# Attention and a low-rank mixer on one core: scores three key blocks at a time, with a PSUM bank pair taken from other uses

## The chip, the core and the metric

The kernel runs on one core of a Trainium2 chip. A core has TensorE (PE in the profile; its weight loads are shown apart as PEld), VectorE (DVE), ScalarE (ACT), GpSimd (POOL) and SyncE (SP, which here only issues transfers). TensorE writes its results to PSUM, and VectorE or ScalarE must read them out of there; this reading out is called an eviction below. The metric is the time of one execution on the device, in microseconds (us). Before the change it is 588.72 us, the median of three runs (587.74 to 589.25).

## What is computed

Cut to what matters, in NumPy terms:

```python
# q, k, v: (8 batches, 12 heads, 448 positions, 64); g_q, g_k: (64,)
q_n, k_n = rmsnorm(q) * g_q, rmsnorm(k) * g_k      # over the last axis
attn = softmax(q_n @ k_n^T / 8)                    # 448 x 448 for each head
x = attn @ v                                       # laid out as (8, 448, 768)
u = x + (x^T @ U @ V)^T                            # U: (448, 32), V: (32, 448)
out = u + relu(u @ w_ch1) @ w_ch2                  # w_ch1: (768, 3072), w_ch2: (3072, 768)
```

So there are 48 pairs of heads (six for each batch), and each batch ends in a two-layer network of width 3072. The matmuls of that network are most of the work.

## The kernel before

The attention of batch b+1 is woven into the network of batch b: `mlp(b)` is a generator that gives one chunk of six matmuls at a time, and `weave` puts the pieces of the attention between chunks according to their weights. The instructions of each engine then run in the order in which the code names them.

PSUM is held by three pools. All small and large results other than scores take turns in `ps_mm`.

```python
ps_mm = ctx.enter_context(tc.tile_pool(name="ps_mm", bufs=3, space=bass.MemoryType.PSUM))  # one bank each
ps_s = ctx.enter_context(tc.tile_pool(name="ps_s", bufs=2, space=bass.MemoryType.PSUM))    # two banks each
ps_r = ctx.enter_context(tc.tile_pool(name="ps_r", bufs=1, space=bass.MemoryType.PSUM))    # 1/rms, one bank
...
rs_bank = ps_r.tile([SP, 6 * 16], FP32, name="rs_bank")
```

The scores of one pair of heads come in four key blocks (kc = 0 to 3) of 112 keys. One block is two matmuls, one for each head; the head dimension is 64, so that each uses 64 of the 128 rows. ScalarE takes the exponential of a block straight from PSUM.

```python
def scores(p, kcs):
    flat, n = k_side(p), SP if p == 0 else P
    for kc in kcs:
        sc = ps_s.tile([P, 2, 512], FP32, tag="s", name="sc")
        c = (2 * kc + 1) * SP
        for hh in range(2):
            pp = slice(hh * D, (hh + 1) * D)
            nc.tensor.matmul(sc[0:n, hh, 0:S], flat[pp, c:c + n], blocks(p)[pp, :, 0], start=True, stop=True)
        scs[p, kc] = sc

def expo(p, kc):
    nc.scalar.activation(Es[p % NE][:, :, PAD + kc * S:PAD + (kc + 1) * S], scs.pop((p, kc))[0:SP, :, 0:S],
                         AF.Exp, scale=float(D) ** 0.5)
```

`values` makes the product with v for one head: 16 matmuls with 65 columns into a tile `o`, then three VectorE instructions that divide by the sum. `mix_t` and `mix_x` are the mixer (tiles `pm`, `px`), `transposes` fills a tile `pt`. All of these tiles, and those of the network, `ph` and `po`, are in `ps_mm`.

```python
def values(p, hh):
    o = ps_mm.tile([P, 4, D + 1], FP32, tag="mm", name="o")
    products(p, hh, o)       # 16 matmuls
    normalize(p, hh, o)      # reciprocal and two multiplications on VectorE

def mix_t(b, cols):
    t4, pms = t_of(b), []
    for c in cols:
        pms.append(ps_mm.tile([P, c.stop - c.start], FP32, tag="mm", name="pm"))
        mix_to(pms[-1], b, c)                      # 4 matmuls
    for c, pm in zip(cols, pms):
        nc.vector.tensor_copy(t4[:, c], pm)

def mix_x(b, i, half):
    px = ps_mm.tile([P, HALF], FP32, tag="mm", name="px")
    ...                                            # 1 or 2 matmuls
    nc.vector.tensor_tensor(xt, px, xt, OP.add)

def mlp(b):
    ...
    for hc in range(KH):                           # 24 tiles ph of 384 or 512 columns
        ph = ps_mm.tile([P, n], FP32, tag="mm", name="ph")
        for dc in range(done, KD):                 # 6 matmuls: one chunk
            nc.tensor.matmul(ph, w1b[:, dc, hc * P:(hc + 1) * P], u[:, dc, :], ...)
        if (hc % 3 if b else hc % 2 == 0 or hc < 5):
            nc.scalar.activation(hT[:, hc, 0:n], ph, AF.Relu)
        else:
            nc.vector.tensor_relu(hT[:, hc, 0:n], ph)
        yield n
    for i, half, w0, w1 in parts:                  # 6 or 8 tiles po of 384 columns
        po = ps_mm.tile([P, w1 - w0], FP32, tag="mm", name="po")
        for hc in range(KH):                       # 24 matmuls: four chunks
            nc.tensor.matmul(po, hT[:, hc, i * P:(i + 1) * P], w2b[:, half, hc, w0:w1], ...)
            if hc % 6 == 5 and hc != KH - 1:
                yield w1 - w0
        nc.vector.tensor_add(osb[:, cols], po, xt[i][:, cols])
        ...
```

In the attention, pairs 6 to 47 are woven in; for each, the scores are asked for twice, two blocks each time.

```python
add(2 if 6 < p <= 12 else 1, scores, p, (0, 1))
add(0, expo, p, 0)
...
add(0 if alone else 1, expo, p, 1)
if p % 6:
    add(1, values, p - 1, 0)
...
add(2 if alone else 1, scores, p, (2, 3))
...
add(0, expo, p, 2)
if p % 6:
    add(1, values, p - 1, 1)
...
add(0 if early else 1, expo, p, 3)
```

Pairs 0 to 5, the first batch, are written out by hand in a head of their own. There, three tiles of `ps_mm` serve as `bank0` to `bank2`.

Of the kernel before, what the change touches and what calls it, by code (L numbers as in the profile page):

```python
# [9 lines left out]
FP32 = mybir.dt.float32  # L10
# [7 lines left out]
def kernel(  # L18
# [20 lines left out]
    P = 128  # L39
    NJ = 4  # L40
    SP = S // NJ
# [6 lines left out]
    NT, NP = B * 3, B * 6  # L48
# [13 lines left out]
    consts = ctx.enter_context(tc.tile_pool(name="consts", bufs=1))  # L62
    norm = ctx.enter_context(tc.tile_pool(name="norm", bufs=2))
    upool = ctx.enter_context(tc.tile_pool(name="upool", bufs=1))
    opool = ctx.enter_context(tc.tile_pool(name="opool", bufs=3))
    ps_mm = ctx.enter_context(tc.tile_pool(name="ps_mm", bufs=3, space=bass.MemoryType.PSUM))
    ps_s = ctx.enter_context(tc.tile_pool(name="ps_s", bufs=2, space=bass.MemoryType.PSUM))
    ps_r = ctx.enter_context(tc.tile_pool(name="ps_r", bufs=1, space=bass.MemoryType.PSUM))

    shift = consts.tile([P, 3 * P], BF16, name="shift")  # L70
    ident = shift[:, P:2 * P]
# [25 lines left out]
    qkL = [consts.tile([P, 2, 2, 2, NJ * D], FP32, name=f"qk{i}") for i in range(2)]  # L97
    vL = [consts.tile([P, HG, NJ * D], FP32, name=f"vt{i}") for i in range(2)]

    rs_bank = ps_r.tile([SP, 6 * 16], FP32, name="rs_bank")  # L100

    def rs_of(p, n=1, of=rs_bank):

        c = 16 * (p % 6)
        return of[:, c:c + 16 * n]

    spare = hT.rearrange("p k n -> p (k n)").bitcast(FP32)

# [108 lines left out]
    def reduce(p, hs=ALL):  # L217
        nc.vector.tensor_reduce(rs_of(p, of=sums).rearrange("p (s h j) -> p s h j", s=2, h=2)[:, :, hs],  # L218
                                sqs[p].rearrange("p (s h j d) -> p s h j d", s=2, h=2, d=D)[:, :, hs], AX, OP.add)

    def rsqrt(p, n=1):
        rs = rs_of(p, n)
        nc.scalar.activation(rs, rs_of(p, n, sums), AF.Ln, bias=eps)
        nc.scalar.activation(rs, rs, AF.Exp, scale=-0.5)  # L224
# [10 lines left out]
    def k_side(p):  # L235

        return qkTs[3] if p == 0 else qkTs[p % NQ]

    def blocks(p):
        return qkTs[p % NQ][:, 0:SQK].rearrange("p (j s r) -> p j s r", j=NJ, s=2)  # L240
# [28 lines left out]
    def scores(p, kcs):  # L269
        flat, n = k_side(p), SP if p == 0 else P  # L270
        for kc in kcs:
            sc = ps_s.tile([P, 2, 512], FP32, tag="s", name="sc")
            c = (2 * kc + 1) * SP
            for hh in range(2):
                pp = slice(hh * D, (hh + 1) * D)
                nc.tensor.matmul(sc[0:n, hh, 0:S], flat[pp, c:c + n], blocks(p)[pp, :, 0],  # L276
                                 start=True, stop=True)
            scs[p, kc] = sc
# [152 lines left out]
    def attention(b):  # L431
        items = []

        def add(weight, fn, *args):
            items.append((weight, lambda: fn(*args)))

        for p in range(b * 6, b * 6 + 6):
            t, odd = divmod(p, 2)
            early = p < 12
            if p == 12:  # L440
                add(0, gains, p)
            add(2 if 6 < p <= 12 else 1, scores, p, (0, 1))
            add(0, expo, p, 0)
            if p == 11:
                add(0, touch, 7)
                add(0, load, 7)
                add(0, load_v, 7)
            elif early and odd:
                add(0, rsqrt, p + 1, 2)
                add(0, scale, p + 1)  # L450
            elif early and p > 6:
                add(0, scale, p + 1)
            elif p >= 12 and p + 2 < NP:
                add(0, scale, p + 2)
                add(0, dma_transposes, p + 2)
            alone = p >= 12 and p % 6 == 0
            add(0 if alone else 1, expo, p, 1)
            if p % 6:
                add(1, values, p - 1, 0)
            if t + 2 < NT:  # L460
                for a in range(2):
                    if odd and p > 11 or p == 11 and a == 0:
                        add(0, reduce, 2 * t + 4 + a if p > 11 else 12)
                    elif not odd and not early:
                        add(0, squares, 2 * t + 4 + a)
            add(2 if alone else 1, scores, p, (2, 3))
            if early and not odd:
                add(0.5, transposes, p + 1)
                if p < 10:
                    add(0, reduce, p + 2)  # L470
            add(0, expo, p, 2)
            if p % 6:
                add(1, values, p - 1, 1)
            if early and not odd:
                if p < 10:
                    add(0, reduce, p + 3)
                for a in range(2):
                    if p != 8:
                        add(0, squares, (10 if p == 6 else 12) + a)
            if odd and p > 11 and t + 3 < NT:  # L480
                add(0, load, t + 3)
                add(0, load_v, t + 3)
            if not odd and t + 1 < NT:
                add(0, cast_v, t + 1)
            if p + 1 < NP and p > 11:
                add(0, gains, p + 1)
            add(0 if early else 1, expo, p, 3)
            if early and odd and p < 11:
                add(1, transposes, p + 1)
            if p == 9:  # L490
                add(0, touch, 6)
                add(0, load, 6)
                add(0, load_v, 6)
            if odd and p > 11 and t + 2 < NT:
                add(0, rsqrt, 2 * t + 4, 2)
        add(1, values, b * 6 + 5, 0)
        add(1, values, b * 6 + 5, 1)
        return items
# [53 lines left out]

    def head():
        warm, rsb = (ps_s.tile([P, 2, 512], FP32, tag="s", name="sc") for _ in range(2))
        banks = [ps_mm.tile([P, 512], FP32, tag="mm", name=f"bank{i}") for i in range(3)]
        held = {}
        copies = {"a": nc.scalar.copy, "v": nc.vector.tensor_copy}
        rs0 = [rs_bank[:, 0:8], rsb[0:SP, 0, 0:8]]
        sums0 = [sums[:, 0:8], sums[:, 8:16]]
        FIRST, REST = slice(0, 1), slice(1, NJ)  # L560

# [11 lines left out]
        def op(name, p, n, how):  # L573
# [45 lines left out]
            elif name in ("Ek", "El"):  # L619
                js = slice(0, NJ) if p else FIRST if name == "Ek" else REST  # L620
                take_k(p, turned(("T" if p else "T" + name[1], p)), copies[how], js)
            elif name == "SC":
                scores(p, (n,))
            elif name == "X":
                expo(p, n)
# [35 lines left out]
        for word in HEAD.split():  # L661
            word, _, how = word.partition(":")
            name = word.rstrip("0123456789")
            digits = word[len(name):]
            p = int(digits[0]) if digits else 0
# [7 lines left out]
    with tc.manual_schedule():  # L673
# [12 lines left out]
        load_v(2)  # L686
        setup()
        head()
        load(5)
        load_w2(0, 2)  # L690
# [5 lines left out]
        for b in range(B):  # L696
            fill = mlp(b)
            if b == 0:
                for _ in range(5):
                    next(fill)  # L700
                transposes(6)
                load_v(5)
                next(fill)
                extra = [(0, lambda i=i, h=h: mix_x(0, i, h)) for i in range(3) for h in range(2)]
                items = attention(1)
                step = len(items) // 7
                for n, x in enumerate(extra):
                    items.insert((n + 1) * step + n, x)
                weave(fill, volume(0) * 0.585, items)
                squares(14)  # L710
                squares(15)
                items = mixing(1)
                items[3:3] = [(0, lambda: reduce(13)), (0, lambda: rsqrt(12, 2))]
                weave(fill, volume(0) * 0.135, items)
                for a in range(2):
                    scale(12 + a)
                    dma_transposes(12 + a)
                for a in range(2):
                    reduce(14 + a)
                rsqrt(14, 2)  # L720
                load(8)
                load_v(8)
            elif b + 1 < B:
                weave(fill, volume(b % 2) * 0.72, attention(b + 1))
                weave(fill, volume(b % 2) * 0.135, mixing(b + 1))
# [32 lines left out]
```

## Time and profile before

| what | before |
|---|---|
| median time of three runs | 588.72 us |
| span of the profiled execution | 585.9 us |
| PE busy | 578.7 us |
| DVE busy | 294.3 us |
| ACT busy | 264.1 us |
| POOL busy | 125.8 us |
| granted TensorE clock, mean over the span | 1.00 |

The profile is that of one execution. A group's row gives the source line, the engine, what it writes and reads, how often, its busy time and the mean of one. Matmuls overlap in a pipeline: one with 512 columns is shown with 377 to 390 ns from start to end, though the next one starts some 216 ns after it. So the time that a matmul costs is read from one start to the next, not from its length. Timeline rows merge equal instructions that follow each other: start, length, engine, line, names, count, and in brackets how long the engine was idle before and what ended that.

### The profile page before, as it was taken

To read this page: it belongs to the slowest core of one execution; us is meant where nothing else is said; L and a number is where in the kernel's file an instruction comes from. 1 tells how busy PE (TensorE), PEld (TensorE's weight loads), DVE (VectorE), ACT (ScalarE), POOL (GpSimd) and SP (SyncE) were. 2 spreads that over 40 slices of the span, in tenths; PEclk is the share of its full clock that TensorE was granted. 3 is DMA by queue.
4 is the path that set the end of the run, shared out by engine and by line. 5 is a ranking of instruction groups with operands and counts; after the bars stand their busy time and mean duration, and the time that the engine had idled before them with its cause. 6 is when DMAs were issued, how large, how long until landed. Compare 5 with 4: busy or idle time off the path is not lost.

```text
span 585.9 us, 11336 instructions
## 1 busy us (share of the span) xinstructions
PE 578.7 (99%) x4749; PEld 319.3 (54%) x4749; DVE 294.3 (50%) x601; ACT 264.1 (45%) x427; POOL 125.8 (21%) x111
## 2 busy tenths in 40 slices
PE   8999999999999999999999999999999999999997
PEld 3665555445655556444565556544565555554565
DVE  6968767445544557355443656454454452521111
ACT  7966531666206761366511774066630576112200
POOL 5955041423200333031130330302312000000000
PEclk9999999999999999999999999999999999999999
DMA  8999995914543445454154642651454410140011
GB/s 281 277 245 233 204 283 130 293 33 124 152 95 93 116 130 159 101 140 124 43 152 97 153 139 66 168 134 50 140 142 93 63 33 2 41 95 0 1 54 55
DMA packets 108274, 72.26 MB, mean 123 GB/s; under 512 B 56656, under 2 KB 104768, under 8 KB 108224
## 3 DMA queue, kind: packets, MB, share of 16 engines
q1 hardware_dynamic: 96544, 61.50, 40.1%
q0 software_dynamic: 11008, 9.44, 10.0%
q8 instruction: 37, 0.61, 0.4%
q10 hardware_dynamic: 672, 0.61, 0.4%
q14 instruction: 13, 0.11, 0.1%
HBM read 56.78 MB, written 11.01 MB: 116 GB/s over the span
## 4 chain that ended last, share of the span: by engine, by line
PE 94%; DVE 2%; DMA 2%; SPq 0%; issue 0%; ACT 0%; DVEq 0%
PE ph L392 38%; PE po L416 37%; PE o L289 7%; PE sc L276 7%; PE px L362 1%; DMA Vf<-in_moe_V_dram 1%; DMA qk<-in_q_dram 1%; PE bank L289 1%; PE sc L529 1%; SPq L184 0%; DVE osb L420 0%; DVE qkn L229 0%; PE pt L244 0%; DVE sums L218 0%; DVE qkT L248 0%
## 5 line engine op out<-in xcount | busy, mean ns | idle before, releaser
L281 ACT ACTIVATE E<-sc 112x896 bf16<-112x896 f32 x192 | 171.4, 914 | 156.9 <-PE sc L276 156.8
L416 PE MATMUL po<-w2b,hT 128*128 128x384 bf16 (+1 forms) x1368 | 237.8, 323 | 1.0 <-DVE osb L420 0.8
L416 PEld LDWEIGHTS <-hT 128*128 128x128 bf16 x1368 | 128.5, 98 | 88.3 <-issue 11.0
L392 PEld LDWEIGHTS <-w1b 128*128 128x128 bf16 x1128 | 102.7, 98 | 106.2 <-issue 20.3
L215 POOL TENSOR_TENSOR sq<-qk 112x1024 f32<-112x1024 f32 x42 | 79.4, 1894 | 308.6 <-DMA qk<-in_k_dram 223.2
L392 PE MATMUL ph<-uB,w1b 128*128 128x512 bf16 x576 | 132.4, 379 | 0.0
L395 ACT ACTIVATE hT<-ph 128x512 bf16<-128x512 f32 (+1 forms) x122 | 66.8, 547 | 105.6 <-PE ph L392 104.6
L392 PE MATMUL ph<-uA,w1b 128*128 128x384 bf16 x552 | 100.3, 326 | 0.1
L397 DVE TENSOR_SCALAR hT<-ph 128x384 bf16<-128x384 f32 (+1 forms) x66 | 41.1, 622 | 89.8 <-PE ph L392 89.7
L289 PEld LDWEIGHTS <-E 112*128 112x128 bf16 x1536 | 60.8, 98 | 15.4 <-issue 1.9
L289 PE MATMUL o<-va,E 112*128 112x65 bf16 x1344 | 56.9, 194 | 0.0
L229 DVE TENSOR_TENSOR qkn<-qk,rs_bank 112x1024 bf16<-112x1024 f32 x45 | 54.3, 1213 | 3.5 <-ACT rs_bank L224 3.4
L276 PE MATMUL sc<-qkT 64*128 64x448 bf16 x376 | 54.0, 355 | 0.4 <-DVE qkT L251 0.2
L301 DVE RECIPROCAL rec<-o 128x4 f32<-128x4 f32 x84 | 15.2, 181 | 76.2 <-PE o L289 76.0
L218 DVE TENSOR_REDUCE sums<-sq 112x16 f32<-112x1024 f32 x43 | 50.5, 1208 | 0.6 <-ACT gcol L656 0.4
L420 DVE TENSOR_TENSOR osb<-po,xe 128x384 f32<-128x384 f32 x32 | 17.8, 557 | 40.5 <-PE po L416 40.1
L420 DVE TENSOR_TENSOR osb<-po,xo 128x384 f32<-128x384 f32 (+1 forms) x25 | 13.5, 542 | 43.1 <-PE po L416 43.1
L276 PEld LDWEIGHTS <-qkT 64*128 64x128 bf16 (+1 forms) x384 | 12.6, 94 | 32.9 <-issue 26.6
L364 DVE TENSOR_TENSOR xe<-px,xe 128x384 bf16<-128x384 f32 x32 | 17.8, 556 | 14.7 <-PE px L362 9.1
L201 POOL CAST va<-vt 112x1024 bf16<-112x1024 f32 x23 | 23.9, 1043 | 2.5 <-DMA vt<-in_v_dram 1.8
L267 ACT ACTIVATE qkT<-qkT,gg 128x448 bf16<-128x448 bf16 x36 | 23.8, 661 | 0.0
L309 DVE TENSOR_TENSOR xe<-o,rec 64x64 bf16<-64x64 f32 x84 | 18.3, 218 | 0.7
(92 smaller groups left out, 210.9 us busy)
## 6 DMA issues: line engine op xcount, KB each, us to landing
qk<-in_q_dram SPq DMA_DIRECT2D x44, 256.0 KB, 4.3
qk<-in_k_dram SPq DMA_DIRECT2D x44, 256.0 KB, 4.7
vt<-in_v_dram SPq DMA_DIRECT2D x22, 512.0 KB, 5.7
w1b<-in_moe_w_ch_dram POOLq DMA_DIRECT2D x6, 768.0 KB, 20.3
w2b<-in_moe_w_ch_dram POOLq DMA_DIRECT2D x6, 768.0 KB, 33.2
out_dram<-osb SPq DMA_DIRECT2D x7, 336.0 KB, 2.8
out_dram<-osb SPq DMA_DIRECT2D x8, 288.0 KB, 3.0
out_dram<-osb SPq DMA_DIRECT2D x8, 240.0 KB, 2.7
```

The source lines that it names most:

```text
L201: nc.gpsimd.tensor_copy(vas[t % NV][:, :, :, 0:D], v_of[t][0:SP].rearrange("p h (j d) -> p h j d", d=D))
L215: nc.gpsimd.tensor_tensor(dst, src, src, OP.mult)
L218: nc.vector.tensor_reduce(rs_of(p, of=sums).rearrange("p (s h j) -> p s h j", s=2, h=2)[:, :, hs], sqs[p].rearrange("p (s h j d) -> p s h ...
L229: nc.vector.tensor_tensor(qkns[p].rearrange("p j g d -> p g j d"), qk_of[t][0:SP, a].rearrange("p s h (j d) -> p (s h) j d", d=D), rs_of(p ...
L276: nc.tensor.matmul(sc[0:n, hh, 0:S], flat[pp, c:c + n], blocks(p)[pp, :, 0], start=True, stop=True)
L281: nc.scalar.activation(Es[p % NE][:, :, PAD + kc * S:PAD + (kc + 1) * S], scs.pop((p, kc))[0:SP, :, 0:S], AF.Exp, scale=float(D) ** 0.5)
L289: nc.tensor.matmul(o[:, i, :], E[:, hh, c:c + P], va[:, hl, kc, :], start=(kc == 0), stop=(kc == NJ - 1))
L392: nc.tensor.matmul(ph, w1b[:, dc, hc * P:(hc + 1) * P], u[:, dc, :], start=(dc == 0), stop=(dc == KD - 1))
L395: nc.scalar.activation(hT[:, hc, 0:n], ph, AF.Relu)
L397: nc.vector.tensor_relu(hT[:, hc, 0:n], ph)
L416: nc.tensor.matmul(po, hT[:, hc, i * P:(i + 1) * P], w2b[:, half, hc, w0:w1], start=(hc == 0), stop=(hc == KH - 1))
L420: nc.vector.tensor_add(osb[:, cols], po, xt[i][:, cols])
```

## The change

Scores are now asked for three key blocks at a time, counted across the pairs (block number 4p + kc), from pair 6 on, the first of batch 1. The aim is to let TensorE turn less often from the network's matmuls, which use 128 rows, to those of the scores, which use 64, and back. Three blocks need three places in PSUM: the third of each three goes into a fixed two-bank tile, `third`. To make room, `ps_mm` has two banks in place of three, and the bank that held 1/rms is gone: for pairs 0 to 7 1/rms lies in the second half of `third`, and from pair 8 on in SBUF. The head uses the first half of `third` as its third bank. Some pieces move along: the transposes for pairs 8 and 10 and the gains of the next pair come earlier, because the first block of the next pair may now be asked for together with the last ones of this pair. The short title of the change also speaks of scaling on GpSimd; in the code, `scale` stays on VectorE, and only the place of 1/rms changes.

```diff
-    ps_mm = ctx.enter_context(tc.tile_pool(name="ps_mm", bufs=3, space=bass.MemoryType.PSUM))
+    ps_mm = ctx.enter_context(tc.tile_pool(name="ps_mm", bufs=2, space=bass.MemoryType.PSUM))
     ps_s = ctx.enter_context(tc.tile_pool(name="ps_s", bufs=2, space=bass.MemoryType.PSUM))
-    ps_r = ctx.enter_context(tc.tile_pool(name="ps_r", bufs=1, space=bass.MemoryType.PSUM))
+    ps_x = ctx.enter_context(tc.tile_pool(name="ps_x", bufs=1, space=bass.MemoryType.PSUM))
...
-    rs_bank = ps_r.tile([SP, 6 * 16], FP32, name="rs_bank")
-    def rs_of(p, n=1, of=rs_bank):
+    third = ps_x.tile([P, 2, 512], FP32, name="third")
+    rms = consts.tile([SP, 6 * 16], FP32, name="rms")
+    def rs_of(p, n=1, of=None):
         c = 16 * (p % 6)
-        return of[:, c:c + 16 * n]
+        return (of or (third[0:SP, 1] if p < 8 else rms))[:, c:c + 16 * n]
...
         for kc in kcs:
-            sc = ps_s.tile([P, 2, 512], FP32, tag="s", name="sc")
+            if p > 5 and (4 * p + kc) % 3 == 2:
+                sc = third
+            else:
+                sc = ps_s.tile([P, 2, 512], FP32, tag="s", name="sc")
...
+        def run(p, kc):
+            i = 4 * p + kc
+            if i % 3 == 0:
+                add(1, three, i)
+            add(0 if i % 3 == 0 else 1, expo, p, kc)
+
+        def three(i):
+            for j in range(i, i + 3):
+                scores(j // 4, (j % 4,))
...
-            add(2 if 6 < p <= 12 else 1, scores, p, (0, 1))
-            add(0, expo, p, 0)
+            run(p, 0)
...
-            alone = p >= 12 and p % 6 == 0
-            add(0 if alone else 1, expo, p, 1)
+            run(p, 1)
...
-            add(2 if alone else 1, scores, p, (2, 3))
...
-            add(0, expo, p, 2)
+            if early and odd and p < 11:
+                add(0.5, transposes, p + 1)
+            if p + 1 < NP and p > 11:
+                add(0, gains, p + 1)
+            run(p, 2)
...
-            if p + 1 < NP and p > 11:
-                add(0, gains, p + 1)
-            add(0 if early else 1, expo, p, 3)
-            if early and odd and p < 11:
-                add(1, transposes, p + 1)
+            run(p, 3)
...
-        banks = [ps_mm.tile([P, 512], FP32, tag="mm", name=f"bank{i}") for i in range(3)]
+        banks = [ps_mm.tile([P, 512], FP32, tag="mm", name=f"bank{i}") for i in range(2)] + [third[:, 0]]
...
-        rs0 = [rs_bank[:, 0:8], rsb[0:SP, 0, 0:8]]
+        rs0 = [third[0:SP, 1, 0:8], rsb[0:SP, 0, 0:8]]
```

## The prediction, made before the changed kernel had run

> **What bounds the kernel now.** I read the page first: busy time by engine and the chain that ended last.
>
> ```profile
> span 585.9 us, 11336 instructions
> PE 578.7 (99%) x4749; PEld 319.3 (54%) x4749; DVE 294.3 (50%) x601; ACT 264.1 (45%) x427; POOL 125.8 (21%) x111
> ...
> PE 94%; DVE 2%; DMA 2%; SPq 0%; issue 0%; ACT 0%; DVEq 0%
> PE ph L392 38%; PE po L416 37%; PE o L289 7%; PE sc L276 7%; PE px L362 1%; DMA Vf<-in_moe_V_dram 1%; DMA qk<-in_q_dram 1%; PE bank L289 1%; PE sc L529 1%; SPq L184 0%; DVE osb L420 0%; DVE qkn L229 0%; PE pt L244 0%; DVE sums L218 0%; DVE qkT L248 0%
> ```
>
> TensorE sets the time; VectorE and ScalarE are busy half of it. So whatever makes TensorE's stream shorter counts in full, and so does every wait put into it. Next I read the timeline of TensorE with its evicting engines, in one stretch of batch 3:
>
> ```profile
> 248.58 0.55 PE L276 MATMUL sc<-qkT 64*128 64x448 bf16 x4
> 249.06 2.76 PE L392 MATMUL ph<-uB,w1b 128*128 128x512 bf16 x12
> 251.66 0.68 PE L289 MATMUL o<-va,E 112*128 112x65 bf16 x16
> 251.87 0.69 DVE L397 TENSOR_SCALAR hT<-ph 128x512 bf16<-128x512 f32 x1 [2.66 <-PE ph L392]
> 252.18 1.46 PE L392 MATMUL ph<-uB,w1b 128*128 128x512 bf16 x6
> 252.47 0.17 DVE L301 RECIPROCAL rec<-o 128x4 f32<-128x4 f32 x1
> 252.68 0.36 DVE L306 TENSOR_TENSOR xe<-o,rec 128x192 bf16<-128x192 f32 x1
> 252.95 0.20 DVE L309 TENSOR_TENSOR xe<-o,rec 64x64 bf16<-64x64 f32 x1
> ```
>
> Two things are to be seen. Two score blocks hold TensorE from 248.58 to 249.06. And the last `ph` before the `o` is free again only at 251.87 + 0.69 = 252.56, which is 0.90 us after TensorE has gone on to `o` at 251.66; `o` itself takes 0.52 us. With three banks the next `ph`, at 252.18, has a bank of its own. Last, the batch's mixer stretch:
>
> ```profile
> 226.90 0.56 DVE L420 TENSOR_TENSOR osb<-po,xe 128x384 f32<-128x384 f32 x1 [0.16 <-PE po L416]
> 226.96 0.33 PE L336 MATMUL pm<-xe,Ub 128*32 128x384 bf16 x1
> ...
> 227.51 1.14 PE L416 MATMUL po<-w2b,hT 128*128 128x384 bf16 x6 [0.21 <-DVE osb L420]
> ...
> 231.08 0.49 PE L362 MATMUL px<-t4b,V 128*128 128x384 bf16 x2
> 231.44 1.02 DVE L364 TENSOR_TENSOR xo<-px,xo 128x384 bf16<-128x384 f32 x2 [0.58 <-PE px L362]
> ```
>
> At 227.51 three banks already do not suffice: `po` waits until `osb` is written (227.46), starts 0.05 us after that, and TensorE has lost 0.21 us. By the waits this occurs only four times (0.8 us in all); it is what every short reuse of a bank looks like.
>
> **What the Trainium skill says.** (1) TensorEngine Tiling (Array Packing), section Key Properties: changing the tiling mode, as from 128 rows to 64, drains TensorE. The trace agrees: the first score matmul starts 311 ns after the last 512-column `ph` matmul, where within `ph` it is 216, and 258 after a 384-column one, where it is 163: 95 ns lost. Within a score group the matmul pairs start 3 to 4 ns apart and the second pair at 200 ns; the group of four ends at 485 ns, so another 85 ns go on the way back. (2) TensorE: Matmul & The Clock Gate, section Back-to-back issue gap: N / 2.4 + 2.5 ns, that is 215.8 and 162.5 for 512 and 384 columns; the trace has the same. (3) PSUM — Partial Sum Buffer, section Specifications: eight banks in a partition. The pools before hold 3 + 4 + 1, those after 2 + 4 + 2: the bank for `third` can only come from `ps_mm`. (4) The same page's Summary: evacuate promptly. Here the evictions are prompt, and they still end 0.6 to 1.0 us after TensorE has moved on.
>
> **The gain.** In the order of the built kernels, pairs 6 to 47 have 84 groups of four score matmuls before and 56 of six after. A group of four costs 95 + 485 = 580 ns; one of six should cost 95 + 485 + 200 = 780. That is 84 x 0.580 = 48.7 us against 56 x 0.780 = 43.7: 5.0 us saved, all of it on the path. The 1/rms in SBUF is read by a VectorE instruction of 1.21 us that bounds nothing; I give it nothing.
>
> **The cost: two banks in place of three.** For every `ps_mm` tile I took from the trace when its eviction ends, counted from the start of TensorE's next work: 0.69 us for `ph` on ACT with 384 columns, 0.80 with 512; 0.76 and 0.89 on DVE; 1.01 for `o`; 0.76 for `px` and for `po` (0.67 when mixer matmuls follow); 0.88 for `pm`. These scatter little. A reuse starts 0.05 us after that, as seen at 227.51. From the built changed kernel I took which bank each tile gets, and what TensorE does between the last matmul of a tile and the next tile in the same bank. If that is shorter, TensorE stands still for the difference. Before, the shortest such gaps are about 0.6 to 0.7 us, six in all, among them the four waits above. After:
>
> - An `o` (0.52 us) between two tiles in one bank, 50 times. `ph` on ACT, 384 columns: 13 x (0.69 + 0.05 - 0.52) = 2.9 us. DVE, 384: 11 x 0.29 = 3.2. ACT, 512: 9 x 0.33 = 3.0. DVE, 512: 9 x 0.42 = 3.8. `po`: 8 x 0.29 = 2.3. Together 15.2.
> - The mixer. `px` directly after `px` in one bank: 8 x (0.76 + 0.05) = 6.5. `po`, one `px` (0.16), `po`: 10 x (0.81 - 0.16) = 6.5. `pm` directly after `pm`: 3 x 0.93 = 2.8. `po`, `pm` (0.35), `pm`: 4 x 0.37 = 1.5, and the `po` behind it 4 x 0.21 = 0.8. Together 18.1.
> - Batch 1 only: three reuses with one `px` between, 0.58 + 0.65 + 0.90, and five with a transposed tile (0.45) between, 0.29 + 2 x 0.36 + 2 x 0.61. Together 4.2.
> - `o`, one 384-column chunk (0.98), next tile: 20 in the second layer x 0.08 = 1.6; and where VectorE had a 1.2 us reduction or scaling in front of an `o` (four of 84 before, ending 1.65 to 2.17 us late), 4 x 0.9 = 3.6. Together 5.2.
>
> The sum is 42.7 us. It counts each wait as if the ones before it had not happened, while a wait gives the evicting engines time to catch up; I take off an eighth, which is a choice, and put 37. The score banks: before a group's third block, the exponential of the previous third must be done. Where no `values` lie between (the start of each batch) and a chunk has 384 columns, TensorE has 0.69 + 3 x 0.98 = 3.6 us between thirds' rounds, and ACT has three exponentials (2.74) and one or two relus (0.5 each); I add 0.5 us for four batches, 2 us. Total: 588.7 - 5.0 + 37 + 2 = 622.7, say 623.
>
> **Rivals.** (a) The waits are mostly hidden, because VectorE and ScalarE are half idle: then only the gain stays, 584 us. For it: the kernel has 99% PE and evictions that never hurt. Against it: a half-idle engine still needs 0.7 to 0.9 us for one eviction, and 0.52 or 0.16 us between reuses is less; 227.51 shows TensorE standing still in this very case. (b) The waits chain up: with two banks, one held for four chunks by a `po`, everything else goes through the other, and each 1.2 us VectorE instruction in front of an eviction is felt by TensorE. Then the last item of the sum is two or three times as large and nothing is taken off: 640 us. For it: reductions and scalings, some 90 of 1.2 us each. Against: at 252.18 the eviction comes before the reduction in VectorE's queue, and only four of 84 `o` were late. (c) ACT becomes the bound where attention is woven in. By stages it is busy 31.86 of 49 us from 177 to 226, 65%; three score places in place of two even loosen it. It would add a few us at the batch starts and no more.
>
> **Range and chances.** Rival (a) in part, with half of the waits hidden, gives 588.7 - 5 + 20 = 604; (b) gives 640. I take 605 to 640 as the range. Slower by over 2% means above 600.5, that is, over 17 us of waits left from 42.7; the parts that hold without any queue, 15.2 + 18.1, alone are 33. I give slower 0.93, within 2% 0.05, faster 0.02.
>
> **What would show it.** Right: score groups of six that last about 0.685 us, 56 of them; PE busy down, and new PE idle time of 30 to 45 us ended by DVE and ACT, on `ph` and `po` and on `px` and `pm`, each of 0.2 to 0.9 us; the stretch from 520 us on, where no attention is woven in, unchanged in length. The prediction is wrong if TensorE's idle time on the network's tiles stays under 15 us, if a group of six lasts as long per block as before, or if the head (the first 70 us) grows by more than 2 us, of which I put in nothing.

## The result and the profile after

The changed kernel takes 639.36 us (median of four runs, 638.64 to 640.12) against 588.71 us for the kernel before: a ratio of 1.086, with a 95% interval of 1.084 to 1.088. That is 50.7 us more; foreseen were 34.3 (623 us), in a range of 605 to 640.

The page of the changed kernel, the lines that answer to those of before:

```profile
span 636.7 us, 11300 instructions
PE 591.2 (93%) x4749; PEld 328.1 (52%) x4749; DVE 304.0 (48%) x601; ACT 264.4 (42%) x427; POOL 131.4 (21%) x111
...
PE 77%; ACT 12%; DVE 9%; issue 2%; DMA 1%; SPq 0%; ACTq 0%
PE po L421 34%; PE ph L397 30%; ACT E L286 6%; ACT hT L400 4%; PE sc L281 4%; PE o L294 3%; DVE hT L402 2%; DVE osb L425 2%; PE third L281 2%; DVE sums L220 1%; PE px L367 1%; ACT qkT L269 1%; DVE xo L369 1%; DMA qk<-in_k_dram 1%; DVE qkn L231 1%
```

The chain that ended last now goes through ScalarE and VectorE for 21% of the span, in place of 2%: TensorE's stream is broken by evictions and exponentials. TensorE's waits, by what ended them:

```profile
PE po L421 <- DVE osb L425: 8.8, 13, 1.4
PE px L367 <- DVE xo L369: 5.6, 8, 1.1
PE ph L397 <- ACT hT L400: 4.1, 17, 0.5
PE ph L397 <- DVE hT L402: 4.1, 12, 1.1
PE third L281 <- ACT E L286: 3.3, 7, 0.7
PE pt L246 <- DVE hT L402: 2.9, 1, 2.9
PE pm L341 <- DVE t4b L350: 2.0, 3, 0.7
```

Most of these are waits for a bank (us in all, times, longest); the one of `pt` is for the most part another kind, as is shown further down. They add up to less than was lost, for a reason that is worth knowing: in these profiles busy time runs to the end of a matmul's pipeline, so a matmul with nothing behind it is shown busy for 0.33 to 0.38 us where its neighbours follow after 0.16 or 0.22. Each wait hides some 0.16 us of itself in busy time. PE busy even rose, from 578.7 to 591.2, while the time in which PE is not busy rose from 7.2 to 45.5. What was lost has to be counted from one matmul's start to the next. The `o` between two `ph` in one bank, in the timeline of the changed kernel:

```profile
281.90 0.67 PE L294 MATMUL o<-va,E 112*128 112x65 bf16 x16
...
282.10 0.69 DVE L402 TENSOR_SCALAR hT<-ph 128x512 bf16<-128x512 f32 x1 [3.29 <-PE ph L397]
...
282.84 1.46 PE L397 MATMUL ph<-uB,w1b 128*128 128x512 bf16 x6 [0.27 <-DVE hT L402]
```

Here `ph` starts 0.94 us after `o`, in place of 0.52: a loss of 0.42 us, of which the bracket shows 0.27. The eviction ends at 282.79, and `ph` follows 0.05 us later. And `px` behind `px`, then `po` behind `po` with one `px` between, in the mixer:

```profile
258.81 0.33 PE L367 MATMUL px<-t4b,V 128*128 128x384 bf16 x1
259.18 0.56 DVE L369 TENSOR_TENSOR xo<-px,xo 128x384 bf16<-128x384 f32 x1 [0.58 <-PE px L367]
259.79 0.32 PE L367 MATMUL px<-t4b,V 128*128 128x384 bf16 x1 [0.65 <-DVE xo L369]
...
260.92 0.33 PE L367 MATMUL px<-t4b,V 128*128 128x384 bf16 x1
...
261.12 0.56 DVE L425 TENSOR_TENSOR osb<-po,xe 128x384 f32<-128x384 f32 x1 [0.42 <-PE po L421]
...
261.73 0.97 PE L421 MATMUL po<-w2b,hT 128*128 128x384 bf16 x5 [0.49 <-DVE osb L425]
```

From 258.81 to 259.79 goes 0.98 us for a matmul of 0.16.

### The profile page after: what moved, and what is told of

The parts are those of the page before. It is cut to its first block, busy times and chain, and to the rows that moved or that the text cites. A ratio compares the mean times of both kernels' runs of the same rounds, so it can differ in the third digit from the quotient of the medians.

```text
span 636.7 us, 11300 instructions
## 1 busy us (share of the span) xinstructions
PE 591.2 (93%) x4749; PEld 328.1 (52%) x4749; DVE 304.0 (48%) x601; ACT 264.4 (42%) x427; POOL 131.4 (21%) x111
## 4 chain that ended last, share of the span: by engine, by line
PE 77%; ACT 12%; DVE 9%; issue 2%; DMA 1%; SPq 0%; ACTq 0%
PE po L421 34%; PE ph L397 30%; ACT E L286 6%; ACT hT L400 4%; PE sc L281 4%; PE o L294 3%; DVE hT L402 2%; DVE osb L425 2%; PE third L281 2%; DVE sums L220 1%; PE px L367 1%; ACT qkT L269 1%; DVE xo L369 1%; DMA qk<-in_k_dram 1%; DVE qkn L231 1%
## 5 line engine op out<-in xcount | busy, mean ns | idle before, releaser
L286 ACT ACTIVATE E<-sc 112x896 bf16<-112x896 f32 x136 | 122.2, 917 | 165.9 <-PE sc L281 165.8
L397 PEld LDWEIGHTS <-w1b 128*128 128x128 bf16 x1128 | 107.1, 98 | 118.8 <-issue 26.7
L217 POOL TENSOR_TENSOR sq<-qk 112x1024 f32<-112x1024 f32 x42 | 81.1, 1937 | 348.0 <-DMA qk<-in_k_dram 184.9
L397 PE MATMUL ph<-uB,w1b 128*128 128x512 bf16 x576 | 131.0, 379 | 4.0 <-DVE hT L402 2.4
L231 DVE TENSOR_TENSOR qkn<-qk,rms 112x1024 bf16<-112x1024 f32 x40 | 56.2, 1407 | 8.6 <-ACT rms L226 8.3
L306 DVE RECIPROCAL rec<-o 128x4 f32<-128x4 f32 x84 | 15.2, 181 | 80.8 <-PE o L294 80.6
L286 ACT ACTIVATE E<-third 112x896 bf16<-112x896 f32 x56 | 51.4, 918 | 2.3 <-PE o L294 1.8
L281 PE MATMUL sc<-qkT 64*128 64x448 bf16 x264 | 38.7, 358 | 0.4 <-DVE qkT L253 0.2
L281 PEld LDWEIGHTS <-qkT 64*128 64x128 bf16 (+1 forms) x384 | 15.7, 95 | 35.9 <-issue 25.9
L203 POOL CAST va<-vt 112x1024 bf16<-112x1024 f32 x23 | 27.9, 1216 | 1.3 <-DMA vt<-in_v_dram 1.3
```

Of the source, the lines that this page charges most:

```text
L217: nc.gpsimd.tensor_tensor(dst, src, src, OP.mult)
L231: nc.vector.tensor_tensor(qkns[p].rearrange("p j g d -> p g j d"), qk_of[t][0:SP, a].rearrange("p s h (j d) -> p (s h) j d", d=D), rs_of(p ...
```

## The experiments

The theory: TensorE waits because two `ps_mm` banks come back too late (bank theory). The rivals: asking for three blocks at a time costs the time, or VectorE, slowed by 1/rms in SBUF, does.

**Two banks alone.** The kernel before, with

```diff
-    ps_mm = ... tc.tile_pool(name="ps_mm", bufs=3, ...)
+    ps_mm = ... tc.tile_pool(name="ps_mm", bufs=2, ...)
```

and a third bank for the head from a pool of its own.

> The kernel before with two ps_mm banks in place of three, and nothing else (the head keeps a third bank of its own). Bank theory: TensorE gets the same waits on evictions that the changed kernel shows on the tiles of the network, of o and of the mixer, 40 to 48 us, and no gain from longer score groups: 630 us (622 to 638). Rival, that the longer score groups or the place of 1/rms cost the time: 589 to 595 us.

Measured: 630.17 us, ratio 1.070 (1.067 to 1.073), 40.8 us more. TensorE's waits in that run:

```profile
PE po L417 <- DVE osb L421: 6.5, 12, 0.8
PE px L363 <- DVE xo L365: 5.6, 8, 1.1
PE ph L393 <- DVE hT L398: 4.2, 11, 1.4
PE ph L393 <- ACT hT L396: 2.4, 11, 0.5
PE pm L337 <- DVE t4b L346: 2.0, 3, 0.7
```

They are the waits of the changed kernel again, except for those of `third` and `pt`. The bank theory holds: four fifths of the loss come from this one edit.

**1/rms in SBUF alone.** The kernel before, with

```diff
+    rms = consts.tile([SP, 6 * 16], FP32, name="rms")
-    def rs_of(p, n=1, of=rs_bank):
+    def rs_of(p, n=1, of=None):
-        return of[:, c:c + 16 * n]
+        return (of or (rs_bank if p < 8 else rms))[:, c:c + 16 * n]
```

> The kernel before with 1/rms in SBUF from pair 8 on, and nothing else. Bank theory: VectorE's scaling takes up to 2 or 3 us where GpSimd works beside it, as in the changed kernel, but with three banks TensorE hardly waits for it: 588 to 591 us. Rival, that the slower scaling is a main cost of the change: 600 us and more.

Measured: 589.31 us, ratio 1.000 (0.999 to 1.002). The scaling does get slower (up to 2.88 us in place of 1.22), and TensorE does not feel it. As a cause by itself this rival is out.

**The mixer's tiles elsewhere.** The changed kernel, with

```diff
-            pms.append(ps_mm.tile([P, c.stop - c.start], FP32, tag="mm", name="pm"))
+            pms.append(ps_s.tile([P, 2, 512], FP32, tag="s", name="sc")[:, 0, 0:c.stop - c.start])
...
-        px = ps_mm.tile([P, HALF], FP32, tag="mm", name="px")
+        if b == 0:
+            px = ps_mm.tile([P, HALF], FP32, tag="mm", name="px")
+        else:
+            px = ps_s.tile([P, 2, 512], FP32, tag="s", name="sc")[:, 0, 0:HALF]
```

> The changed kernel with the mixer's tiles pm and px of batches 1 to 7 in the two score places (idle in those stretches) in place of the two ps_mm banks. Bank theory: the waits of px on px, po on px and pm on pm go, some 16 us of the 18 that the trace of the changed kernel shows for them: 622 us (619 to 627). Rival, that the waits only move, because VectorE is behind anyway in these stretches: 633 us and more.

Measured: 619.84 us, that is 19.5 us less than the changed kernel. The waits of `px` and `pm` are gone from the list, and those of `po` fall from 8.8 to 4.0 us; hardly anything took their place. What is saved is about what the trace of the changed kernel shows for the mixer (17.5 us, in the table below).

**A stiff third bank for `o`.** The kernel with two banks, with

```diff
-        o = ps_mm.tile([P, 4, D + 1], FP32, tag="mm", name="o")
+        o = ps_b.tile([P, 512], FP32, tag="b", name="o")[:, 0:4 * (D + 1)].rearrange("p (i d) -> p i d", i=4)
```

where `ps_b` has one bank (in the head it is the third one).

> The kernel before with its three ps_mm banks dealt out stiffly: two for everything but o, the third for o alone. Bank theory: against the kernel with two banks (630.2 us), the waits with an o between two tiles go (14.2 on ph, 3.2 on po, 1.2 on px in its trace, and part of 6.1 of ph on ph), the mixer's 18 us stay: 610 us (605 to 615). Rival, that one lost bank of three costs 40 us wherever it is taken: 625 us and more.

Measured: 611.84 us, 18.3 us less than with two banks, though it has as many banks as the kernel before, which is 23 us faster. In its list the waits of `ph` for the relus fall from 6.6 to 1.0 us, and those of the mixer are as they were:

```profile
PE px L363 <- DVE xo L365: 5.6, 8, 1.1
PE po L417 <- DVE osb L421: 4.9, 10, 0.5
```

So the two large terms of the sum, `o` and mixer, are each removed by giving their tiles another place. It is not the number of banks alone that counts, but the time until the same one is needed again.

**Scaling on GpSimd.** The changed kernel, with

```diff
-        nc.vector.tensor_tensor(
+        (nc.gpsimd if p >= 8 else nc.vector).tensor_tensor(
             qkns[p].rearrange("p j g d -> p g j d"),
```

> The changed kernel with the scaling of pairs 8 to 47 on GpSimd, so that VectorE loses 40 instructions of 1.2 to 2.9 us. If VectorE's long instructions in front of evictions are what made the change cost more than foreseen, the waits of 2.9 us in batch 0 (with the slow TensorE clock after it) and of 1.6 us in the second layers go: 626 us (622 to 632). If they matter little: 637 to 641 us. A third way: GpSimd, with 40 times 1.9 us more, is late for the transposes, and the time grows.

Measured: 640.83 us, no gain. VectorE is busy for 250 us in place of 304, and the waits on `po`, `px`, `pm` and on the relus are the same to 0.1 us. Only two others moved: the one at pair 8 grew from 2.9 to 4.2 us as GpSimd is late with the scaling, and `ph` behind the division of an `o` fell from 1.4 to 0.8. So the scaling in VectorE's queue is not what makes the evictions late. The 47 reductions of 1.2 us stayed on VectorE; no run took them away.

**Four single banks.** Three blocks at a time with a bank gained and not lost: the first block of each three takes two tiles of a four-bank `ps_mm`, and has one exponential for each head.

```diff
-    ps_mm = ... bufs=2     # and ps_x with third
+    ps_mm = ... bufs=4
...
-            if p > 5 and (4 * p + kc) % 3 == 2:
-                sc = third
+            if p > 5 and (4 * p + kc) % 3 == 0:
+                sc = [ps_mm.tile([P, 512], FP32, tag="mm", name="s1") for _ in range(2)]
```

> Three key blocks at a time, but with four single ps_mm banks: the first block of each three takes two of them, with one exponential for each head, the other two blocks the two score places; 1/rms has a ps_mm bank up to pair 7 and SBUF after that. In its built order hardly any tile comes back to a bank within 1 us. Bank theory: the 40 us of bank waits go, the longer score groups save 5.7 us, and the waits on exponentials inside the groups, 7 us in the changed kernel, stay in part: 587 us (583 to 591). Rival, that asking for three blocks at a time costs much by itself: 595 us and more.

Measured: 590.18 us, ratio to the kernel before 1.0024 (1.0013 to 1.0036). The bank waits are gone, and with them 49.2 of the 50.7 us. What is left is in the score groups and in batch 1, whose attention is woven into the first layer of batch 0 (34.0 us in place of 30.5):

```profile
PE sc L281 <- ACT E L291: 3.6, 8, 0.7
PE pt L245 <- DVE qkn L230: 1.8, 1, 1.8
```

**Gains on VectorE.** The same, with

```diff
-        nc.scalar.activation(qT, qT, AF.Copy, scale=gg)
+        nc.vector.tensor_scalar(qT, qT, gcol[:, 0:1], gcol[:, 1:2], OP.mult, OP.mult)
```

> The same with the gains of pairs 12 to 47 on VectorE in place of ScalarE, 36 x 0.67 us less on ScalarE. If the waits inside the score groups come from ScalarE's queue (exponential, gains, relu, exponential), they shrink by 3 to 5 us: 583 us (580 to 586). If not, it stays where the kernel with four single banks is.

Measured: 618.56 us, ratio 1.050 (1.047 to 1.053), a miss. The instruction is short there in 28 of 36 cases (0.38 to 0.40 us) and takes 1.97 to 2.09 us in the other eight, and it stands in VectorE's queue, where the scores wait for it:

```profile
PE sc L281 <- DVE qkT L268: 21.3, 11, 3.8
```

At each of the seven waits of 1.5 us or more, one or two reductions of 1.2 us stand just before the gain in that queue; at the longest (3.83 us, at 199.87) two reductions take 2.34 us, and then the gain itself 2.09. After six of the seven TensorE also runs slow (see the last section).

**Four single banks, scaling on GpSimd.** The edit of the scaling above, in the kernel with four single banks.

> Four single banks with the scaling of pairs 8 to 47 on GpSimd, as the short title of the change has it. VectorE loses 40 x 1.2 us or more; with few bank waits left there is little to gain, and the scaling of pair 8 may come late, as it did in the changed kernel with this edit (4.2 us of waiting): 588 us (583 to 594).

Measured: 597.11 us, ratio 1.013 (1.011 to 1.016), above the range. The transposes of pair 8 wait 6.2 us for GpSimd, and TensorE runs slow after that.

**From batch 2 on.** Batch 1 is woven as in the kernel before; three blocks with four single banks begin with pair 12. 1/rms stays in a `ps_mm` bank up to pair 13, which is then given back.

```diff
-            if p > 5 and (4 * p + kc) % 3 == 0:
+            if p > 11 and (4 * p + kc) % 3 == 0:
...
+            if p % 6 == 0:
+                add(0, gains, p + 1)
             run(p, 0)
...
-            if p + 1 < NP and p > 11:
+            if p + 1 < NP and p > 11 and p % 6:
                 add(0, gains, p + 1)
```

> Batch 1 as in the kernel before (two blocks at a time, 1/rms in PSUM up to pair 13); from batch 2 on three blocks at a time with four single ps_mm banks, and the gains of the second pair of each batch moved ahead of the batch's first scores, where ScalarE is idle. If the gain of the longer groups (0.8 us a batch) was eaten by batch 1 and by ScalarE's queue at the batch starts (1.04 us every other batch), the kernel is faster than before: 585 us (582 to 587). If the waits on exponentials only move to the next group, 588 to 590 us.

Measured: 585.11 us, ratio to the kernel before 0.994 (0.991 to 0.996; measured beside it, that kernel took 589.61): a small gain, and the fastest of all here. TensorE's longest waits for other engines outside the head are now these:

```profile
PE sc L281 <- ACT qkT L268: 0.6, 3, 0.2
...
PE sc L281 <- ACT E L291: 0.3, 1, 0.3
```

The edit changes two things at once, since there is a fourth `ps_mm` bank besides the longer groups. In the traces the stretch from the first network tile to the last matmul is 3.9 us shorter than before (540.7 against 544.6), and 2.8 of them are in the score groups; the rest is mostly mixer waits that three banks had left.

**All gains earlier.** The same, with `add(0, gains, p + 1)` ahead of `run(p, 0)` for every pair.

> The same, with the gains of every next pair ahead of the first scores of its forerunner. If the remaining waits in the groups (0.27, 0.53 and 0.62 us in two batches) come from gains just ahead of a group, they go too: 583 us (581 to 586). If they come from the exponentials and relus alone, no difference to the other kernel (within 1 us).

Measured: 586.64 us, ratio 0.996 (0.994 to 0.997), not the 2 us foreseen; the two intervals overlap, so it is not shown to be slower either. By stages of the trace the later second layers of 384-column batches are 0.1 to 0.3 us shorter, but the first layer of batch 1, where attention starts with pair 12, is 2.1 us longer (40.9 against 38.8); most of that is one wait of 1.5 us, at 114.81, for a relu that now stands in ScalarE's queue behind a gain whose input came late.

## Why the prediction was right in direction and short in size

Counted from one matmul's start to the next, less the shortest time that the same step takes in either trace, the terms of the sum are:

| term | foreseen, us | in the changed kernel's trace, us |
|---|---|---|
| `o` between two tiles of a bank (13.7 before `ph`, 6.0 before `po`, 0.5 before `pt`, 0.2 before `px`), with late ones and `po` before `o` (0.5) | 15.2 + 5.2 | 20.9 |
| mixer (`px` on `px` 6.9, `po` behind `px` 6.2, `pm` and the `po` behind it 4.4; less the waits of before) | 18.1 | 17.5 |
| batch 1, `px` or transposed tile between | 4.2 | 5.4 |
| taken off because waits give the others time | -5.7 | 0 |
| transposes of pair 8, waiting for their input | 0 | 2.4 |
| inside score groups | 2 | 6.8 (7.4 less 0.6 before) |
| longer score groups | -5.0 | -5.7 |
| growth of the head | 0 | 2.3 |
| slow clock after that wait of pair 8 | 0 | 2.4 |

The right column adds up to 52.0, against 50.7 measured; rows that are counted against the shortest step each overlap a little.

- **The bank waits** were right, in sum and nearly one by one. The 42.7 us (the terms of batch 1 add up to 4.4 and not to the 4.2 in it) stand against 43.8. In the trace of the kernel with two banks alone the same count gives 42.6, and that edit costs 40.8 us.
- **The deduction of an eighth** was the largest miss. It supposed that a wait lets the evicting engines catch up with later ones. But most of these evictions have no queue before them: they are late by their own latency, and the next one is as late again. `px` directly after `px` lost 0.87 us in each of eight places, against 0.81 foreseen. That taking the scaling off VectorE changes none of these waits fits this, and so does that the two large terms can be removed one at a time, by 19.5 and 18.3 us.
- **The gain** was right: a group of six lasts 674 ns where nothing holds it up, against 685 foreseen, and there are 56.
- **The score places** were mis-sized, 2 us for 6.8. The third block of a group needs the exponential of the third before it, and ahead of that ScalarE has two exponentials, relus and, at the batch starts of every other batch, a gain of 0.67 us that the change had put just there. The group then lasts 0.87 us longer, as at 207.49 us in the changed kernel's trace, three times in all. (The 1.04 us in one of the expectations is the whole step to the third block, of which some 0.2 us is the normal one.) Rival (c) had foreseen a few us at the batch starts; its reason against, that a third place loosens ScalarE's hold, did not hold. With this gain moved ahead of the batch and batch 1 left out, the waits in groups fall from 7.5 us in the trace of four single banks to 2.7, and the time by 5.1 us.
- **The transposes of pair 8** were not in the sum at all. They wait 2.9 us in batch 0, and it looks like a wait for a bank, since the relu named in the list ended last. But the weight load of the same transposes shows that their input came only at 55.33; the bank added the last 0.46 us:

```profile
53.21 2.07 DVE L231 TENSOR_TENSOR qkn<-qk,rms 112x1024 bf16<-112x1024 f32 x1 [2.64 <-ACT rms L226]
55.33 0.10 PEld L246 LDWEIGHTS <-qkn 112*128 112x128 bf16 x1 [2.60 <-DVE qkn L231]
...
55.79 0.91 PE L246 MATMUL pt<-shift,qkn 112*128 112x112 bf16 x8 [2.94 <-DVE hT L402]
```

The change asks for these transposes earlier, while their scaling still waits for 1/rms and then takes 2.07 us in place of 1.21. With four single banks and the same order 1.8 us of this wait stay; with two banks alone and the old order there is none. TensorE then ran slow.
- **Nothing for the head** was wrong by 2.3 us in these two traces: the first network tile starts at 40.2 us in place of 37.9. This scatters: the three traces with this head have 40.2, 40.6 and 43.1 us, the nine others 37.4 to 39.8. There `third` serves both 1/rms and the third bank, and TensorE now waits 0.8 and 0.5 us for ScalarE to write 1/rms; nothing was run to settle the rest.
- **The signs.** One that the prediction had named against itself came true: what stood in the first 70 us grew by more than 2 us. The head and the first layer of batch 0 end at 83.2 us in place of 68.4. Of this, 12.5 us are in that layer (43.0 us in place of 30.5; 39.1 with two banks alone; 30.5 in the kernel that starts with pair 12). PE busy did not go down either; the reason is given with the waits above. The others came as foreseen: PE idle time grew by 38 us, and the last batch's two layers, where no attention is woven in, last 31.1 and 31.4 us in both traces.
- **Luck.** The 639.36 us lie 0.64 us inside the range, whose end was the 640 of rival (b). Half of (b) held: nothing was to be taken off. Its other half, long VectorE instructions in front of evictions that double or triple the last item of the sum, did not: the row of `o` has 20.9 us for 20.4. The time came near 640 through terms that neither the sum nor (b) had at their size: score places, transposes of pair 8, head, slow clock. That the range held is luck in this respect.

Of the 9.2 us between two banks alone and the whole change, the score groups, the head and the wait for pair 8's input with the slow clock after it come to some 14 us by the table, and the longer groups give 5.7 back. Their exact shares were not separated by a run.

## What to carry to other kernels

When buffers are taken away, list for every buffer what the producer does until it needs the same one again, and set that against eviction latency (here 0.6 to 1.0 us after the producer has moved on); the difference is lost each time, whatever the evicting engine's share of busy time. Do not take anything off such a sum for catching up unless a queue is what makes the eviction late. When a piece is moved earlier, look for its input as well as for its buffer. And a saving on the bound engine of some 1% is worth having only if it costs none of these waits: here it came out once no bank was lost, the batch starts were relieved of a gain and the crowded first batch was left alone.

## What the runs showed of the hardware that was not expected

A long wait costs more than itself. After the 2.9 us in batch 0, TensorE's granted clock was 0.53 for six us. The stretches from 52, 56 and 62 us of the changed kernel (length, then busy time of PE, PEld, DVE, ACT, POOL, the clock, and DMA):

```profile
52.00:56.00 4.00, 1.06 (x22) 0.96 (x20) 2.76 (x4) 1.95 (x4) 3.70 (x2) 0.85 1.18 245
56.00:62.00 6.00, 6.00 (x32) 2.61 (x30) 1.82 (x5) 1.41 (x2) 1.22 (x2) 0.53 1.31 204
62.00:83.00 21.00, 17.28 (x177) 9.97 (x173) 14.14 (x31) 9.57 (x16) 0.00 (x0) 1.00 1.06 165
```

TensorE is busy all the time from 56 to 62 and does 32 matmuls; 384-column ones start 320 ns apart in place of 163. The Trainium skill, TensorE: Matmul & The Clock Gate, section Why this matters for your kernels, says to keep idle gaps below about 3 us; here 2.9 us was already too long, while a wait of 1.8 us at the same place in the kernel with four single banks left the clock at 1.00. In the kernel with the gains on VectorE even 2.13 us was too long, twice. After the first of these, which ended at 351.28:

```profile
352.00:355.00 3.00, 3.00 (x25) 1.82 (x24) 0.37 (x2) 1.29 (x3) 2.57 (x2) 0.50 0.59 201
```

In all twelve traces, past the head, each of the ten waits of 2.1 us or more was followed within 4 us by matmuls at half pace, and none of the six waits of 1.5 to 1.8 us was. Nothing lies between, so where the limit is stays open.

And the place of an operand changes whether two engines get in each other's way. The scaling on VectorE took 1.21 to 1.22 us with 1/rms in PSUM, also beside GpSimd; with 1/rms in SBUF this is its row:

```profile
L231 DVE TENSOR_TENSOR qkn<-qk,rms x40: 1212/1217/2903, 53.2 to 526.7; 112x1024 bf16<-112x1024 f32 x40
```

The median stays, and the longest is 2.90 us. All ten that took over 1.23 us ran beside GpSimd; three others beside it stayed at 1.22 or 1.23. GpSimd's squares go up to 2.81 us from 1.91. The Trainium skill, SBUF — State Buffer, section Who interferes with whom, says that a VectorE instruction with two inputs in SBUF contends with GpSimd's reads there, and that one with at most one input in SBUF, outside its two-port fast modes, does not. The traces agree with both halves: the first shows in this row, the second in the kernel before, where all 17 scalings beside GpSimd took 1.21 to 1.22 us.
